# Rank of the first weight conversions, engine of the 1 / rms steps of pairs two and three, and lead of the first w3 loads

## Chip, core and metric
One core of a Trainium2 chip runs the whole program. The metric is device time in microseconds (us) of one execution, given as the median of several. Engines are TensorE (PE, with PEld for its weight loads), VectorE (DVE), ScalarE (ACT), GpSimd (POOL) and SyncE (SP, which only issues DMAs here). ScalarE and GpSimd issue DMAs as well.

## The reference
Inputs of the attention are float32, weights float64. `x` below is the attention output with the heads side by side, 1792 x 768.

```
q_n, k_n = rmsnorm(q, g_q), rmsnorm(k, g_k)      # x / sqrt(mean(x*x) + 1e-6) * g
attn = softmax(q_n @ k_n.T / sqrt(64)) @ v       # 4 batches, 12 heads, 448 rows, head size 64
h = x @ w_in;  x = maximum(0.01 * h, h) @ w_out  # 768 -> 2048 -> 768
a, b = x @ w1, x @ w2                            # 768 -> 1024 each
out = ((a * b) @ w3) @ w_last                    # 1024 -> 1024 -> 768
```

`w_last` is the second MLP's `w_out`. The kernel reads the weights as pairs of 32-bit words.

## The kernel before
Every matmul operand is split into a rounded part and a rest (`wh` and `wl`, `kh` and `kl`, `lasth` and `lastl`), and a product is three matmuls. The heads of a batch are worked in 24 pairs. For a pair t, `statistics(t)` makes 1 / rms of q and k: a square and a sum, `rs` by logarithm and exponential on ScalarE, and one small correcting step (lines 160 to 164 on GpSimd, lines 166 to 169 on VectorE for pair zero alone); line 174 then scales the keys. `keys(t)` transposes them (`pk`, L220) and splits them into `kh` (ScalarE, L229) and `kl` (VectorE, L230). `scores(t)` multiplies queries and keys into banks `ps` (L128), VectorE scales a bank and takes its minimum (L265), and ScalarE takes the exponential (L274). The results `p` are transposed into `pt` (L308), copied out as `pth`, and multiplied with the values (`po`).

Between these steps the two last weight matrices are multiplied with each other, w3 @ w_last, by `combine_weights` (banks `pw`, L554). It needs eight tiles of w_last and sixteen half tiles of w3. `Weights` brings them in this order: w_last 0 to 3 (tiles 0 to 3 of its list), the first w3 half (tile 4), then by turns a w_last tile and a w3 half (tiles 5 to 8), w_last 6 and 7 (tiles 9 and 10), and the remaining w3 halves. The first product needs tiles 0 to 4.

Conversion of a tile (`to_float32`) is two ScalarE passes over the words in place (L470, L474) and two VectorE passes into `raw` (L472, L476). `split` then makes hi and lo: for w_last on GpSimd (`lasth` L110, `lastl` L199), for w3 on ScalarE and VectorE (`wh` L505, `wl` L199). Words of w_last lie in a pool of four buffers, those of w3 in a pool `cv3` of five. `Weights.__init__` decides behind which tile's split a load is issued: as early as the buffer allows, and at most seven tiles ahead. A load issued after the first conversion goes to ScalarE's queue, an earlier one to SyncE's.

The order of instructions on each engine is fixed at build time by a list scheduler: among the work that is ready in its own estimate, the one with the higher priority goes first. Code within `tc.high_priority(n)` is ranked n places up: scores 600, statistics 100, and conversions `CONVERT_PRIORITY` = 100 (0 for the very first). On the chip each engine then works through its queue in that order, and waits at each instruction for its inputs and buffers.

Of the kernel before, what the change touches and what calls it, by code (L numbers as in the profile page):

```python
# [28 lines left out]
PB = 2  # L29
KH2 = K2 // 2  # L30
PARTIAL = 3
NO = DM // P
NH = B * H
NS = 1.0 / 2.4
CONVERT_NS = 500.0
CONVERT_PRIORITY = 100
STATS_AHEAD = 2
KEYS_AHEAD = 1
P_TILES = 8
TOGETHER = 2000  # L40
# [9 lines left out]
def attention_then_moe(  # L50
# [90 lines left out]
    def statistics(t):  # L141

        if t >= NH // 2:
            return
        x = pairs[t].pop("rows")
        ss = small.tile([CP, 2, 2, NCH], F32, tag="ss", name="ss", bufs=2)
        after = exps.get(t - STATS_AHEAD) or start.get("keys")
        for part in (1, 0):
            y = x[:, part]
            if part:  # L150
                y = bank("sq")[:CP].rearrange("p (h c d) -> p h c d", h=2, c=NCH)
            with tc.issue_after(after.ins) if after else ExitStack():
                nc.scalar.activation(y, x[:, part], AF.Square)
            nc.vector.tensor_reduce(ss[:, part], y, axis=AX.X, op=ALU.add)
        rs = small.tile([CP, 2, 2, NCH], F32, tag="rs", name="rs", bufs=4)
        y = small.tile([CP, 2, 2, NCH], F32, tag="y", name="y", bufs=2)
        nc.scalar.activation(y, ss, AF.Ln, scale=1.0 / D, bias=eps)
        nc.scalar.activation(rs, y, AF.Exp, scale=-0.5)
        if t:
            nc.gpsimd.tensor_scalar(ss, ss, 0.5 / D, 0.5e-6, op0=ALU.mult, op1=ALU.add)  # L160
            nc.gpsimd.tensor_tensor(y, rs, rs, op=ALU.mult)
            nc.gpsimd.tensor_tensor(y, y, ss, op=ALU.mult)
            nc.gpsimd.tensor_scalar(y, y, 1.0, -1.5, op0=ALU.mult, op1=ALU.add)
            nc.gpsimd.tensor_tensor(rs, y, rs, op=ALU.mult)
        else:
            nc.vector.tensor_scalar(ss, ss, 1.0 / D, 1e-6, op0=ALU.mult, op1=ALU.add)
            nc.vector.scalar_tensor_tensor(y, rs, 0.5, rs, op0=ALU.mult, op1=ALU.mult)
            nc.vector.tensor_tensor(y, y, ss, op=ALU.mult)
            nc.vector.scalar_tensor_tensor(rs, y, -1.5, rs, op0=ALU.add, op1=ALU.mult)
        pairs[t]["scale"] = rs[:, 0]  # L170
        kn = x[:, 0].rearrange("p h c d -> p (h c d)")
        kn = pairs[t]["kn"] = kn.rearrange("p (c h d) -> p c h d", c=NCH, h=2)
        rk = rs[:, 1].unsqueeze(3).to_broadcast([CP, 2, NCH, D])
        nc.vector.tensor_tensor(kn.rearrange("p c h d -> p h c d"), x[:, 1], rk, op=ALU.mult)
# [229 lines left out]
    class Weights:  # L404
# [9 lines left out]
        def __init__(self, sources):  # L414
            self.sources = sources
            self.raw, self.words, self.parts = {}, {}, {}
            self.ready = self.taken = 0
            self.rounded = None
            self.home, self.loads = {}, {}
            last = {"cv": [-4] * 4, "cv3": [-4] * 5}  # L420
            for t, (src, wide, _, _) in enumerate(sources):
                if wide:
                    home = self.home[t] = "cv3" if t < K2 * 3 and self.size(t) < DM else "cv"
                    after = max(last[home].pop(0), t - 7, -4 if t < 5 else 0)
                    self.loads.setdefault(after, []).append(t)
                    last[home].append(t)
            self.pieces = self.work()
            self.after = None
# [102 lines left out]
        def pump(self):  # L531

            if self.after and self.ready == len(self.sources):
                self.after.pump()
            elif self.ready - self.taken < self.AHEAD:
                with tc.high_priority(CONVERT_PRIORITY if self.ready else 0):
                    next(self.pieces, None)

        def take(self):
            while self.ready <= self.taken:  # L540
                with tc.high_priority(CONVERT_PRIORITY if self.ready else 0):
                    next(self.pieces)
            self.taken += 1
            return self.parts.pop(self.taken - 1)
# [18 lines left out]
            yield 3 * n * NS  # L563


    def combine_order():

        early = list(range(KH2))
        late = list(range(KH2, K2))
        yield early, 0, 0  # L570
        for k in range(1, PARTIAL):
            yield [late.pop(0)], k, 0
        yield late, 0, 1
        for k in range(1, PARTIAL):
            yield [], k, 1
        for k in range(PARTIAL, K2):
            yield [], k, 0
            yield [], k, 1

    def combine_weights(ws, pool, hi, lo):  # L580
# [5 lines left out]
        for new, k, half in combine_order():  # L586
            for _ in new:
                while ws.ready <= ws.taken:
                    with tc.high_priority(CONVERT_PRIORITY if ws.ready else 0):
                        next(ws.pieces)  # L590
                    yield CONVERT_NS
                ws.take()
# [159 lines left out]
    last = {}  # L752
# [402 lines left out]
```

## Time and profile before

| | us |
|---|---|
| median of 3 runs | 1183.69 |
| lowest and highest of the 3 | 1180.28 and 1185.77 |
| the profiled execution, its own time | 1182.5 |
| its span, first to last instruction | 1180.7 |
| TensorE busy in the span | 1137.4 |
| VectorE, ScalarE, GpSimd busy | 710.1, 657.7, 243.6 |

The span is the stretch that the trace shows; 1.8 us of the execution's own time lie outside it. An engine that is busy for nearly the whole span sets the time, and what it waits for in the rest is where time can come or go. A timeline row ends, where the engine stood idle before it, with the idle time and the instruction that ended it in brackets.

### The profile page before, as it was taken

What the parts mean: (1) busy time and instruction counts of PE and PEld (TensorE: products, weight loads), DVE (VectorE), ACT (ScalarE), POOL (GpSimd) and SP (SyncE); (2) the same over time, 40 slices, a digit from 0 to 9 for tenths busy, and PEclk for the clock granted to TensorE, in tenths of its full rate; (3) what the DMA queues carried; (4) which work ended last, traced back from release to release, by engine and by line L of the source; (5) the groups of instructions that cost most, each with busy time, mean ns of one, the idle gap of its engine ahead of it and who ended that gap; (6) DMA issues with size and microseconds to landing.
All of it is one profiled execution on the core that took longest, in us unless ns stands there. A gap on an engine that the chain in (4) does not pass through costs nothing.

```text
span 1180.7 us, 16739 instructions
## 1 busy us (share of the span) xinstructions
PE 1137.4 (96%) x6096; PEld 956.8 (81%) x6096; DVE 710.1 (60%) x1334; ACT 657.7 (56%) x1347; POOL 243.6 (21%) x345
## 2 busy tenths in 40 slices
PE   3899999999999999999999999999999999899998
PEld 2678867677787888888888888879999999699997
DVE  7986776877423667567545643483445556954553
ACT  6978687987534566676556643354443344443331
POOL 5632344544212232345222011000000000000000
PEclk8799999999999999999999999999999999999999
DMA  9556565985865446346332421440212212102112
GB/s 315 182 176 221 174 204 193 326 279 186 292 209 162 153 139 206 127 138 200 123 120 95 161 87 43 143 151 28 81 51 57 69 41 78 55 29 89 55 36 103
DMA packets 74979, 164.51 MB, mean 139 GB/s; under 512 B 13968, under 2 KB 42384, under 8 KB 74896
## 3 DMA queue, kind: packets, MB, share of 16 engines
q1 hardware_dynamic: 55392, 80.06, 22.5%
q10 hardware_dynamic: 10800, 48.76, 12.3%
q0 software_dynamic: 8704, 34.61, 7.8%
q8 instruction: 48, 0.79, 0.3%
q14 instruction: 35, 0.29, 0.1%
HBM read 120.46 MB, written 42.95 MB: 138 GB/s over the span
## 4 chain that ended last, share of the span: by engine, by line
PE 84%; DVE 7%; ACT 4%; DMA 3%; issue 1%; ACTq 0%; SPq 0%; POOL 0%; DVEq 0%; POOLq 0%
PE ps_mm L554 32%; PE ps_o L554 13%; PE ps_b L554 9%; PE pt L308 6%; PE ps L128 6%; PE po L128 6%; PE ps_c L554 5%; PE pw L554 5%; PE ps_a L554 2%; DVE ol L199 1%; DMA wh<-kept_first_mlp_h 1%; ACT p L274 1%; DVE wl L199 1%; PE pk L220 1%; ACT w L474 1%
## 5 line engine op out<-in xcount | busy, mean ns | idle before, releaser
L199 DVE TENSOR_TENSOR wl<-raw,wh 128x512 fp32r<-128x512 f32 (+1 forms) x136 | 109.4, 807 | 112.4 <-ACT wh L505 73.5
L265 DVE TENSOR_SCALAR_CACHE_REDUCE p<-ps,rs 112x448 f32<-112x448 f32 x192 | 122.2, 680 | 42.4 <-PE ps L128 42.4
L554 PE MATMUL ps_mm<-xl,wh 128*128 128x448 f32 x384 | 146.2, 381 | 0.0
L554 PE MATMUL ps_mm<-xh,wh 128*128 128x448 f32 x384 | 141.3, 368 | 2.3 <-DMA wh<-kept_first_mlp_h 2.3
L274 ACT ACTIVATE p<-p,low 112x448 f32<-112x448 f32 x192 | 126.5, 662 | 30.1 <-DVE p L265 29.8
L554 PE MATMUL ps_mm<-xh,wl 128*128 128x448 f32 x384 | 141.5, 368 | 0.7 <-DMA wl<-kept_first_mlp_l 0.7
L554 PE MATMUL ps_mm<-gl,wh 128*128 128x448 f32 x288 | 109.5, 381 | 0.0
L554 PE MATMUL ps_mm<-gh,wl 128*128 128x448 f32 x288 | 105.6, 367 | 1.6 <-DMA wl<-kept_first_mlp_l 1.6
L554 PE MATMUL ps_mm<-gh,wh 128*128 128x448 f32 x288 | 106.0, 369 | 1.1 <-DMA wh<-kept_first_mlp_h 1.0
L554 PE MATMUL ps_o<-gl,wh 128*128 128x448 f32 x288 | 104.3, 366 | 0.0
L554 PE MATMUL ps_o<-gh,wl 128*128 128x448 f32 x288 | 100.8, 366 | 0.0
L308 PEld LDWEIGHTS pt<-ident,p 112*112 112x112 f32 x768 | 82.2, 136 | 21.3 <-issue 7.1
L554 PE MATMUL ps_o<-gh,wh 128*128 128x448 f32 x288 | 99.4, 366 | 0.0
L470 ACT ACTIVATE w<-w 128x768 f32<-128x768 f32 (+1 forms) x80 | 63.4, 792 | 64.6 <-DMA w<-w_out 29.7
L308 PE MATMUL pt<-ident,p 112*112 112x112 f32 x768 | 96.2, 265 | 0.0
L505 ACT ACTIVATE wh<-raw 128x512 fp32r<-128x512 f32 (+1 forms) x84 | 59.2, 706 | 56.5 <-PE ps_mm L554 52.6
L554 PEld LDWEIGHTS ps_mm<-xl,wh 128*128 128x128 f32 x384 | 72.4, 189 | 12.5 <-issue 7.2
L476 DVE CUSTOM_DVE_ANT_0 raw<-w,raw 128x1024 uint16<-128x1024 uint16 (+1 forms) x80 | 79.2, 995 | 2.2 <-ACT w L474 0.5
L554 PEld LDWEIGHTS ps_mm<-xh,wh 128*128 128x128 f32 x384 | 72.3, 188 | 9.4 <-issue 3.7
L784 ACT ACTIVATE wh<-raw 128x512 fp32r<-128x512 f32 (+1 forms) x52 | 36.3, 698 | 76.3 <-PE ps_b L554 33.7
L554 PEld LDWEIGHTS ps_mm<-xh,wl 128*128 128x128 f32 x384 | 72.6, 189 | 7.6 <-issue 1.6
L128 PE MATMUL po<-pth,v_sb 112*64 112x448 f32 x384 | 77.5, 545 | 0.0
(141 smaller groups left out, 2530.5 us busy)
## 6 DMA issues: line engine op xcount, KB each, us to landing
w<-w_in ACTq DMA_DIRECT2D x16, 768.0 KB, 5.8
w<-w_out ACTq DMA_DIRECT2D x24, 512.0 KB, 3.9
w<-w ACTq DMA_DIRECT2D x16, 768.0 KB, 4.5
qk_sb<-qk SPq DMA_DIRECT2D x48, 224.0 KB, 4.0
w<-w3t ACTq DMA_DIRECT2D x15, 512.0 KB, 4.6
kept_first_mlp<-raw POOLq DMA_DIRECT2D x16, 384.0 KB, 4.3
kept_first_mlp<-raw POOLq DMA_DIRECT2D x24, 256.0 KB, 3.2
kept_second_mlp<-raw POOLq DMA_DIRECT2D x16, 384.0 KB, 2.9
```

Of the source, the lines that this page charges most:

```text
L128: one = nc.tensor.matmul(out, a, x, start=begin, stop=end)
L199: e.tensor_tensor(out, x, y.bitcast(F32), op=ALU.subtract)
L220: nc.tensor.transpose(pk[:, c * CP : (c + 1) * CP], kn[:, c].rearrange("p h d -> p (h d)"), ident[:CP, :CP],)
L265: nc.vector.tensor_scalar(p, ps[c % 2][e], x["scale"][:, e, c : c + 1], None, op0=ALU.mult, op1=ALU.min, accum_out=low,)
L274: exps[t] = nc.scalar.activation(p, p, AF.Exp, bias=low, scale=-1.0, accum_out=x["sums"][:, e, c : c + 1])
L308: nc.tensor.transpose(pt[:, c * CP : (c + 1) * CP], h["p"][c][:, kc * CP : (kc + 1) * CP], ident[:CP, :CP],)
L470: nc.scalar.activation(h, h, AF.Prelu, scale=2.0**-112, alpha=2.0**32)
L474: self.rounded = nc.scalar.activation(low, low, AF.Copy, scale=2.0**-29)
L476: nc.vector.tensor_tensor(top, top, low, op=ALU.add)
L505: self.rounded = nc.scalar.activation(flat[0], x, AF.Copy)
L554: nc.tensor.matmul(ps[:, :n], a, x, start=begin, stop=end, skip_group_check=on)
L784: nc.scalar.activation(parts[0], x, AF.Copy)
```

## The change
Three things change, and with them the build-time order of the engines' queues.

1. `words_first` ranks the conversions of the first five tiles (`ready <= KH2`, tiles 0 to 4) 1000 places up, above the scores' 600. Before, tile 0 had 0 and the others 100.
2. The correcting step of 1 / rms runs on VectorE for pairs zero, one and two (`POOL_SCALES = 3` counts pairs from zero), before only for pair zero. For the two pairs five GpSimd instructions each become four on VectorE.
3. Loads of the w3 tiles 4, 6 and 8 are issued at most four tiles ahead rather than seven. Tile 4 thereby leaves SyncE's queue, where it stood second among the weight loads, for ScalarE's.

Lines of the attention part move down by 3, those of `Weights` by 4, later ones by up to 7.

```diff
--- before.py
+++ after.py
@@ -29,12 +29,15 @@
 PB = 2
 KH2 = K2 // 2
 PARTIAL = 3
+LATE_WORDS = 4
 NO = DM // P
 NH = B * H
 NS = 1.0 / 2.4
 CONVERT_NS = 500.0
 CONVERT_PRIORITY = 100
+FIRST_WORDS = 1000
 STATS_AHEAD = 2
+POOL_SCALES = 3
 KEYS_AHEAD = 1
 P_TILES = 8
 TOGETHER = 2000
@@ -156,7 +159,7 @@
         y = small.tile([CP, 2, 2, NCH], F32, tag="y", name="y", bufs=2)
         nc.scalar.activation(y, ss, AF.Ln, scale=1.0 / D, bias=eps)
         nc.scalar.activation(rs, y, AF.Exp, scale=-0.5)
-        if t:
+        if t >= POOL_SCALES:
             nc.gpsimd.tensor_scalar(ss, ss, 0.5 / D, 0.5e-6, op0=ALU.mult, op1=ALU.add)
             nc.gpsimd.tensor_tensor(y, rs, rs, op=ALU.mult)
             nc.gpsimd.tensor_tensor(y, y, ss, op=ALU.mult)
@@ -421,7 +424,8 @@
             for t, (src, wide, _, _) in enumerate(sources):
                 if wide:
                     home = self.home[t] = "cv3" if t < K2 * 3 and self.size(t) < DM else "cv"
-                    after = max(last[home].pop(0), t - 7, -4 if t < 5 else 0)
+                    ahead = LATE_WORDS if home == "cv3" and t <= 2 * PARTIAL + 2 else 7
+                    after = max(last[home].pop(0), t - ahead, -4 if t < 5 else 0)
                     self.loads.setdefault(after, []).append(t)
                     last[home].append(t)
             self.pieces = self.work()
@@ -533,12 +537,12 @@
             if self.after and self.ready == len(self.sources):
                 self.after.pump()
             elif self.ready - self.taken < self.AHEAD:
-                with tc.high_priority(CONVERT_PRIORITY if self.ready else 0):
+                with tc.high_priority(words_first(self)):
                     next(self.pieces, None)
 
         def take(self):
             while self.ready <= self.taken:
-                with tc.high_priority(CONVERT_PRIORITY if self.ready else 0):
+                with tc.high_priority(words_first(self)):
                     next(self.pieces)
             self.taken += 1
             return self.parts.pop(self.taken - 1)
@@ -562,6 +566,9 @@
             ws.pump()
             yield 3 * n * NS
 
+
+    def words_first(ws):
+        return FIRST_WORDS if ws.ready <= KH2 else CONVERT_PRIORITY
 
     def combine_order():
 
@@ -586,7 +593,7 @@
         for new, k, half in combine_order():
             for _ in new:
                 while ws.ready <= ws.taken:
-                    with tc.high_priority(CONVERT_PRIORITY if ws.ready else 0):
+                    with tc.high_priority(words_first(ws)):
                         next(ws.pieces)
                     yield CONVERT_NS
                 ws.take()
```

How the queues move is shown at three places. Names with a number after `w_` are weight words; line numbers of the change are the new ones.

VectorE before, from the first scaled scores of pair zero to the scaled keys of pair one (last row):

```order
L265 TENSOR_SCALAR p,low<-ps,rs 112x448 x3
L472 TENSOR_SCALAR raw<-w_299 128x768
L476 ISA raw<-w_299,raw 128x1536
L265 TENSOR_SCALAR p,low<-ps,rs 112x448 x2
L174 TENSOR_TENSOR qk_sb<-qk_sb,rs 112x2x4x64
```

VectorE of the change, the last rows ahead of the scaled keys of pair one (the last two small steps are the rows with `y<-y,ss` and `rs<-y,rs`):

```order
L480 ISA raw<-w_300,raw 128x1536
L171 TENSOR_TENSOR y<-y,ss 112x16
L476 TENSOR_SCALAR raw<-w_302 128x768
L268 TENSOR_SCALAR p,low<-ps,rs 112x448 x2
L172 SCALAR_TENSOR_TENSOR rs<-y,rs 112x16
L480 ISA raw<-w_302,raw 128x1536
L177 TENSOR_TENSOR qk_sb<-qk_sb,rs 112x2x4x64
```

The scaled keys of pair one now stand behind all eight scaled scores of pair zero, behind the conversions of tiles 0 to 3 and behind the four small steps; before they stood behind six scaled scores and tiles 0 and 1.

VectorE before, the rows up to the low part `kl` of pair one's keys (last row):

```order
L476 ISA raw<-w_301,raw 128x1536
L472 TENSOR_SCALAR raw<-w_303 128x768
L472 TENSOR_SCALAR raw<-w_305 128x512
L476 ISA raw<-w_303,raw 128x1536
L476 ISA raw<-w_305,raw 128x1024
L230 SCALAR_TENSOR_TENSOR kl<-pk,gqk,kh 128x448
```

VectorE of the change, the rows between tile 4's conversion and the same `kl` (last row):

```order
L286 TENSOR_SCALAR r<-sum 112x8
L287 RECIPROCAL r<-r 112x8
L157 TENSOR_REDUCE ss<-qk_sb 112x8
L157 TENSOR_REDUCE ss<-sq 112x8
L476 TENSOR_SCALAR raw<-w_355 128x768
L111 COPY pth<-pt 112x448
L480 ISA raw<-w_355,raw 128x1536
L202 TENSOR_TENSOR wl<-raw,wh 128x512
L476 TENSOR_SCALAR raw<-w_461 128x512
L169 TENSOR_SCALAR ss<-ss 112x16
L480 ISA raw<-w_461,raw 128x1024
L233 SCALAR_TENSOR_TENSOR kl<-pk,gqk,kh 128x448
```

Tile 4's conversion (`w_305` before, `w_353` now) is still ahead of `kl`. New ahead of it are the two reciprocal rows, two sums, tiles 5 and 6, a copy `pth`, a rest `wl`, and a small step of pair two.

ScalarE before, around the high part `kh` of pair one's keys (`kh<-pk,gqk`):

```order
L274 ACTIVATE p,sum<-p,low 112x448 x2
L470 ACTIVATE w_303<-w_303 128x768
L474 ACTIVATE w_303<-w_303 128x768
L106 ACTIVATE qh<-qt_sb 128x448
L229 ACTIVATE kh<-pk,gqk 128x448
L274 ACTIVATE p,sum<-p,low 112x448 x2
L153 ACTIVATE sq<-qk_sb 112x512
```

ScalarE of the change, the rows that end with the same `kh`, after the squares of pair two:

```order
L156 ACTIVATE sq<-qk_sb 112x512
L474 ACTIVATE w_355<-w_355 128x768
L478 ACTIVATE w_355<-w_355 128x768
L509 ACTIVATE wh<-raw 128x512
L455 DMA w_483<-w3t 128x1024
L455 DMA w_488<-w3t 128x1024
L474 ACTIVATE w_461<-w_461 128x512
L478 ACTIVATE w_461<-w_461 128x512
L455 DMA w_556<-w3t 128x1024
L160 ACTIVATE y<-ss,eps 112x16
L109 ACTIVATE pth<-pt 112x448 x3
L232 ACTIVATE kh<-pk,gqk 128x448
```

Before, `kh` of pair one stood ahead of the squares of pair two (lines 153 before, 156 now); now it stands behind them, behind the words of tiles 5 and 6, a `wh` and three copies. On TensorE the products of `combine_weights` still begin behind the scores of pair one, in both programs.

## Rows read from the trace of the kernel before

**Rows 1.** Windows of the span: length, busy us of each engine, TensorE clock, DMA.
```profile
0.00:60.00 60.00, 36.36 (x174) 27.47 (x175) 50.52 (x84) 48.81 (x99) 34.28 (x36) 0.83 0.74 248
60.00:1181.00 1121.00, 1100.99 (x5924) 929.30 (x5922) 659.60 (x1251) 608.93 (x1249) 209.29 (x309) 1.00 0.41 133
```

**Rows 2.** Timeline of TensorE, rows with a wait: start, duration, wait.
```profile
21.59 0.98 PE L220 MATMUL pk<-ident,qk_sb 112*128 112x112 f32 x4 [5.77 <-ACT p L274]
...
30.52 0.71 PE L128 MATMUL ps<-kl,qh 64*112 64x448 f32 x2 [3.76 <-DVE kl L230]
...
33.24 0.66 PE L554 MATMUL pw<-lasth,wh 128*128 128x384 f32 x1 [0.34 <-ACT wh L505]
...
42.20 0.45 PE L554 MATMUL pw<-lasth,wh 128*128 128x384 f32 x1 [1.58 <-ACT wh L505]
...
46.88 0.69 PE L554 MATMUL pw<-lasth,wl 128*128 128x384 f32 x1 [2.17 <-DVE wl L199]
```

**Rows 3.** Windows, the two stretches after the first product at half clock.
```profile
33.24:37.00 3.76, 3.76 (x15) 3.56 (x16) 3.76 (x9) 3.76 (x9) 1.14 (x2) 0.50 1.02 390
43.80:50.70 6.90, 4.73 (x16) 3.67 (x15) 6.70 (x10) 6.90 (x14) 2.92 (x3) 0.51 0.25 100
```

**Rows 4.** Timeline of VectorE around pair one: start, duration, instruction.
```profile
12.82 0.56 DVE L472 TENSOR_SCALAR raw<-w 128x768 uint32<-128x768 uint32 x1
...
13.90 0.95 DVE L476 CUSTOM_DVE_ANT_0 raw<-w,raw 128x1536 uint16<-128x1536 uint16 x1
...
29.79 0.67 DVE L230 SCALAR_TENSOR_TENSOR kl<-pk,gqk,kh 128x448 fp32r<-128x448 f32 x1
...
30.39 0.20 DVE L283 TENSOR_SCALAR r<-sum 112x8 f32<-112x8 f32 x1
...
32.42 0.68 DVE L265 TENSOR_SCALAR_CACHE_REDUCE p<-ps,rs 112x448 f32<-112x448 f32 x1
...
34.09 0.69 DVE L199 TENSOR_TENSOR wl<-raw,wh 128x512 fp32r<-128x512 f32 x1
...
35.56 0.42 DVE L472 TENSOR_SCALAR raw<-w 128x512 uint32<-128x512 uint32 x1
...
37.11 2.32 DVE L476 CUSTOM_DVE_ANT_0 raw<-w,raw 128x1024 uint16<-128x1024 uint16 x1
```

**Rows 5.** Timeline of ScalarE from 24 to 36 us.
```profile
24.09 0.61 ACT L229 ACTIVATE kh<-pk,gqk 128x448 fp32r<-128x448 f32 x1
...
29.06 0.60 ACT L153 ACTIVATE sq<-qk_sb 112x512 f32<-112x512 f32 x1 [3.06 <-DMA qk_sb<-qk]
...
30.89 0.92 ACT L470 ACTIVATE w<-w 128x768 f32<-128x768 f32 x1 [0.24 <-DVE r L284]
...
35.45 0.31 ACT L157 ACTIVATE y<-ss,eps 112x16 f32<-112x16 f32 x1
```

**Rows 6.** Timeline of VectorE: small steps, and rows that last long.
```profile
6.92 1.01 DVE L166 TENSOR_SCALAR ss<-ss 112x16 f32<-112x16 f32 x1 [1.19 <-ACT y L157]
7.84 0.16 DVE L167 SCALAR_TENSOR_TENSOR y<-rs 112x16 f32<-112x16 f32 x1
...
8.46 0.69 DVE L174 TENSOR_TENSOR qk_sb<-qk_sb,rs 112x512 f32<-112x512 f32 x1
...
25.78 4.09 DVE L476 CUSTOM_DVE_ANT_0 raw<-w,raw 128x1536 uint16<-128x1536 uint16 x2
...
43.90 2.32 DVE L174 TENSOR_TENSOR qk_sb<-qk_sb,rs 112x512 f32<-112x512 f32 x1 [1.67 <-POOL rs L164]
```

**Rows 7.** Timeline of GpSimd: two subtractions beside those long rows.
```profile
25.66 1.85 POOL L199 TENSOR_TENSOR lastl<-raw,lasth 128x768 fp32r<-128x768 f32 x1
...
43.84 1.83 POOL L199 TENSOR_TENSOR lastl<-raw,lasth 128x768 fp32r<-128x768 f32 x1
```

**Rows 8.** The line of the weight loads, 0 to 40 us: issue, and issue to landing.
```profile
L451 ACTq DMA_DIRECT2D w<-w_last x4: 334/355/444, 15.0 to 30.4; - x4
...
DMA to landing us min/median/max: 4.0/7.8/11.1
```

## The prediction

> **What bounds the kernel now.** I first split TensorE's time by windows [rows 1]: in the first 60 us it is busy for 36.36, after them for 1101.0 of 1121. From 60 us on it runs almost without a pause, and VectorE and ScalarE are busy for less of the time than TensorE is. So a microsecond that TensorE loses in the first 60 us is a microsecond of the span, unless one of the few later pauses takes it up; I count on none of them.
>
> Then I read TensorE's timeline in those 60 us for its waits [rows 2]: 5.77 us before the key transposes of pair one (21.59), 3.76 before the last part of pair one's first scores (30.52, for `kl`), 0.34 before the first product of w3 and w_last (33.24, for `wh`), then 1.58 and 2.17 before the second w3 tile (`wh`, then `wl`). The last granted clock windows after the first product that stand at half speed [rows 3] are from 33.24 to 37.0 and from 43.8 to 50.7: 3.76 and 4.73 us busy at 1.2 rather than 2.4 GHz, so 1.9 and 2.4 us lost, 4.25 together. Both follow pauses.
>
> What TensorE waits for is VectorE and ScalarE: they are busy for 50.52 and 48.81 of the first 60 us [rows 1], with words to convert and scores to scale in one queue each. Every instruction put ahead of `kl` or `kh` in those queues comes out as lateness of the first product, since in both programs the products stand behind the scores of pair one.
>
> **The change part by part.**
>
> *Rank of the first five conversions.* The four w_last tiles and the first w3 tile now go ahead of the scores and of all that follows from them. The scaled keys of pair one fall behind two more scalings, tiles 2 and 3 and four small steps. A tile is 0.56 and 0.95, a scaling about 0.68, a small step about 0.2 (three from 7.84 to 8.46) [rows 4, 6]: 2 x 1.51 + 2 x 0.68 + 0.8 = 5.2, and with neighbouring rows overlapping by 0.07 (29.79 + 0.67 against 30.39 [rows 4]) about 4.7. So the transposes move from 21.59 to about 26.3. That alone is covered: behind them stand the 16 transposes of `p`, under 5 us at the pace of the four key transposes (0.98 [rows 2]), and TensorE then waits for `kh` and `kl` anyway.
>
> The path goes through `kl`. VectorE has these rows newly ahead of it: reciprocals, sums and one copy, 30.39 to 32.42 before, 2.03; tile 5, 1.51; one `wl`, 0.69; tile 6, 0.42 + 0.63 (the 0.95 of a wide tile cut to its two thirds); five small steps, 1.0 [rows 4, 6]. Sum 6.3, less 0.4 of overlap: 5.9, so `kl` would begin at 29.79 + 5.9 = 35.7. Before, it began at 29.79.
>
> ScalarE gives the same date by another way. `kh` stood at 24.09; now it stands behind the squares of pair two, the words of tiles 5 and 6, a `wh`, a logarithm and three copies. Before, that very sequence ran from 29.06 to 35.45 + 0.31, with its first row waiting 3.06 for the q and k rows of pair two [rows 5]. If these land as late as before, `kh` starts at about 35.7 and `kl` 0.6 behind it, 36.3. I take `kl` at 36.0, 6.2 later; the first product then moves from 33.24 to 39.4. **Lost: 6.2.** Bounds: VectorE's rows before `kl` were stretched by 2.5 us in one place alone (two L476 in 4.09 rather than some 1.5 [rows 6]). With that stretch gone the loss is 3.7; with two more such meetings of 1.8 it is 9.8.
>
> What is behind the first product gets better. Tiles 5 and 6 are converted by then: `wh` of tile 6 follows `kh` after two further w_last tiles on ScalarE, 35.7 + 0.6 + 2 x 1.7 = 39.7, and `wl` follows it on VectorE at about 40.5, while the 24 products of the first tile, which ran from 33.24 to 40.62 (42.20 less its wait), would last from 39.4 to 43.1 even in half that time [rows 2]. **Regained: the waits of 1.58 and 2.17, 3.75** [rows 2]. The half clock: after 30.52 TensorE stayed at half until 37.0, 6.5 us [rows 2, 3]. Restarted at 36.7 it would stay there until 43.2, of which 3.8 lie behind the first product: 1.9 lost in place of 4.25. **Regained: 2.3.** Bounds: nothing, if the next pause brings a second half-speed stretch; 4.25 if the restart is at full clock.
>
> *Small steps on VectorE.* For pair two the wait of VectorE for GpSimd (1.67 at 43.90) goes, and its scaled keys need no longer meet a subtraction on GpSimd (2.32 us there, from 43.90 to 46.2, beside a subtraction from 43.84 to 45.67 [rows 6, 7]); that is part of the 2.17 already counted. In its place five new rows per two pairs can meet one: the first step of pair zero took 1.01 and its siblings 0.16 [rows 6]. Behind the first product VectorE still has pair two's scaled keys, three tiles' words, a copy and a `wl` to do before the third w3 tile, and the copy frees a bank for the next scores. Nothing in the trace shows this order. From below such a wait is nothing, from above it is what two of the long rows cost beyond their own 0.6 and 1.5: 1.7 + 2.5 = 4.2 [rows 6]. I take 3.0, nearer the top, since GpSimd makes lo parts of tiles 7, 9 and 10 in just these microseconds. **New waits: 3.0.** The Trainium skill (SBUF — State Buffer, section "Who interferes with whom") says that a VectorE instruction with two SBUF inputs, or one in a two-port mode, is blocked by a GpSimd instruction for its whole length. The row of 2.32 us agrees. By that rule alone each step that meets a subtraction costs up to 1.8 us, and the rival below is its full case.
>
> *Loads.* Tile 4 is no longer loaded from SyncE but from ScalarE, at about 15 us (its first load there was at 15.0), and landings took 4.0 to 11.1 us, mostly 7.8 [rows 8]: 22.8. ScalarE comes to it at about 23.6 (24.09 less its own two passes of 1.1, which stood ahead, plus one exponential). Cost nothing, with 0.8 us of cover; without cover up to 2.5. All words are the same, so later pressure on the queues is unchanged.
>
> **Sum.** +6.2 - 3.75 - 2.3 + 3.0 = +3.2 us on an execution of 1182.5 with a span of 1180.7. The median of the three runs is 1183.7, 1.2 above that execution, so I expect **1187 us**, 0.3% slower. Half a per cent, 5.9 us, is about what a measurement of this kernel can tell from no change (its own three runs differ by 5.5).
>
> **The rivals.**
> - *All is regained.* As forecast, but VectorE is ready with the third tile in time: 6.2 - 6.05 = +0.2, 1184. For it: TensorE has two tiles' products, transposes and scores in that time. Chance 0.16.
> - *The port is the cost.* Three or four small steps or word passes more than before meet a GpSimd subtraction ahead of `kl`, 1.8 each, and the later copies too: +3.2 + 3 x 1.8 = +8.6, 1192. For it: the rows of 1.01 and 2.32. Against it: GpSimd's own ten small steps are gone. Chance 0.20.
> - *The other side: faster.* The stretch in VectorE's queue goes. Ahead of `kl` the two L476 met two GpSimd operations in a row, 2.5 us; the L472 and L476 before them were stretched by the same kind of meeting, and with GpSimd's steps gone they fall between subtractions. With `kl` at 32 (some 4 us sooner than I have it) the first product is at 35.4; 2.2 lost against 6.05 regained and no new wait give -3.9, 1180; with `kl` at 30, -5.9, 1178, which is where it decides. Against it: 5.9 us of rows are newly ahead of `kl`, and ScalarE's sequence holds `kh` as well. Chance 0.14.
> - *The first w3 words are late.* Landing after 11.1 us, ScalarE stands for 2.5 before tile 4, and so does all behind it: +5.7, 1189. Chance 0.06.
>
> **How the numbers follow.** The forecast has chance 0.44; its own range is 1184 to 1190 (the regained clock and the new waits at their bounds do not fall together). Of it a fifth lies over 1189.6, that is 0.09. Slower by over 0.5%: 0.09 + 0.20 x 0.9 + 0.03 = 0.30. Faster by over 0.5%: half of 0.14 and a little for the run's own spread, 0.09. Within: 0.61. The range that leaves out 2 in 10 goes from 1179, into the faster case, to 1194, past the port's.
>
> **What would show it.** Right: pair one's transposes on TensorE after 25 us, its `kh` after 33, the first product at 38 to 41; the waits before the second w3 tile gone; VectorE without a wait for GpSimd before pair two's scaled keys; busy time of TensorE in the first 60 us at 33 to 35 with later windows as before. Wrong: a first product before 36, or pauses of TensorE behind 60 us that before has and the change has not, or the reverse.

## The result and the profile after

| | before | after |
|---|---|---|
| median of 18 runs each, us | 1182.3 | 1188.82 |
| lowest and highest, us | 1178.23 and 1187.37 | 1185.32 and 1193.8 |
| profiled execution, own time and span, us | 1182.5, 1180.7 | 1187.53, 1185.7 |

The ratio after to before is 1.0068 (95% interval 1.0056 to 1.008): 8.0 us slower. The two medians of the table lie 6.5 us apart, a ratio of 1.0055, so the size is known to a microsecond or two. Forecast was +3.2 us, a median of 1187; it counted from the 1183.7 of the first three runs, 1.4 above the median of all 18. The profiled execution of after is a little under its median; its span is 5.0 us longer than that of before.

First TensorE's waits on its timeline after, to be read beside [rows 2]:

```profile
29.37 0.42 PE L223 MATMUL pk<-ident,qk_sb 112*128 112x112 f32 x1 [13.74 <-DVE qk_sb L177]
...
36.11 0.71 PE L131 MATMUL ps<-kh,qh 64*112 64x448 f32 x2 [2.77 <-ACT kh L232]
...
40.38 0.71 PE L131 MATMUL ps<-kl,qh 64*112 64x448 f32 x2 [3.19 <-DVE kl L233]
...
42.15 0.69 PE L558 MATMUL pw<-lasth,wh 128*128 128x384 f32 x1
42.64 0.52 PE L558 MATMUL pw<-lastl,wh 128*128 128x384 f32 x1
42.96 0.52 PE L558 MATMUL pw<-lasth,wl 128*128 128x384 f32 x1
...
44.19 0.34 PE L558 MATMUL pw<-lasth,wh 128*128 128x384 f32 x1
44.36 0.34 PE L558 MATMUL pw<-lastl,wh 128*128 128x384 f32 x1
...
51.40 0.46 PE L131 MATMUL ps<-kh,qh 64*112 64x448 f32 x1 [0.70 <-DVE pth L111]
...
58.97 0.60 PE L223 MATMUL pk<-ident,qk_sb 112*128 112x112 f32 x4 [2.21 <-DVE p L268]
```

The first product of w3 and w_last (L558, L554 before) comes at 42.15, before at 33.24: 8.9 us later. Neither `wh` nor `wl` is waited for behind it any more (1.58 and 2.17 before). New are 0.70 and 2.21, 2.9 together.

What holds that product back is `kl`. VectorE's timeline, the rows of the small steps (L169 to L172), the scaled keys (L177), the reciprocals' first row (L286) and `kl` (L233), beside [rows 4, 6]:

```profile
15.92 1.77 DVE L169 TENSOR_SCALAR ss<-ss 112x16 f32<-112x16 f32 x1
...
20.16 0.79 DVE L170 SCALAR_TENSOR_TENSOR y<-rs 112x16 f32<-112x16 f32 x1
...
23.55 0.16 DVE L171 TENSOR_TENSOR y<-y,ss 112x16 f32<-112x16 f32 x1
...
25.32 1.50 DVE L172 SCALAR_TENSOR_TENSOR rs<-y,rs 112x16 f32<-112x16 f32 x1
...
27.61 1.62 DVE L177 TENSOR_TENSOR qk_sb<-qk_sb,rs 112x512 f32<-112x512 f32 x1
...
30.71 1.79 DVE L286 TENSOR_SCALAR r<-sum 112x8 f32<-112x8 f32 x1
...
37.35 1.79 DVE L169 TENSOR_SCALAR ss<-ss 112x16 f32<-112x16 f32 x1
...
39.66 0.67 DVE L233 SCALAR_TENSOR_TENSOR kl<-pk,gqk,kh 128x448 fp32r<-128x448 f32 x1
```

A small step takes 0.16 us at 23.55, and 0.79, 1.50, 1.77 and 1.79 elsewhere; the reciprocals' first row (L286), 0.20 before, takes 1.79. `kl` stands at 39.66, before at 29.79. GpSimd's timeline shows what ran beside the long rows, beside [rows 7]:

```profile
15.66 2.00 POOL L202 TENSOR_TENSOR lastl<-raw,lasth 128x768 fp32r<-128x768 f32 x1
...
24.96 1.82 POOL L202 TENSOR_TENSOR lastl<-raw,lasth 128x768 fp32r<-128x768 f32 x1
26.74 1.92 POOL L202 TENSOR_TENSOR ql<-qt_sb,qh 128x448 fp32r<-128x448 f32 x1
...
30.33 2.14 POOL L202 TENSOR_TENSOR lastl<-raw,lasth 128x768 fp32r<-128x768 f32 x1
...
37.23 1.88 POOL L202 TENSOR_TENSOR lastl<-raw,lasth 128x768 fp32r<-128x768 f32 x1
```

Each long row of VectorE lies inside or across one of these subtractions: 15.92 in that of 15.66, 25.32 in 24.96, 27.61 in 26.74, 30.71 in 30.33, 37.35 in 37.23. The small steps among them (1.77, 1.50 and 1.79) and the L286 row end within 0.04 us of the end of the subtraction that they meet. The Trainium skill (SBUF — State Buffer, section "Who interferes with whom") says that a VectorE instruction in a two-port mode and a GpSimd instruction compete for a shared pair of ports: whoever issues first has it for its whole instruction, and the other is fully blocked. The trace agrees: steps of 1.77 and 1.79 beside subtractions of 2.00 and 1.88 that began 0.26 and 0.12 us earlier.

On ScalarE the words of tile 4 are converted without a wait for their load, and `kh` starts at 35.41 (forecast 35.7), beside [rows 5]:

```profile
25.49 0.65 ACT L474 ACTIVATE w<-w 128x512 f32<-128x512 f32 x1
...
35.41 0.65 ACT L232 ACTIVATE kh<-pk,gqk 128x448 fp32r<-128x448 f32 x1
```

Windows of after, with the busy time and number of instructions of each engine, then granted clock, DMA share and GB/s, beside [rows 1]:

```profile
0.00:60.00 60.00, 27.56 (x145) 22.07 (x146) 52.43 (x87) 45.61 (x89) 29.95 (x25) 1.00 0.74 245
...
780.00:1000.00 220.00, 217.68 (x1047) 197.87 (x1046) 117.14 (x193) 94.26 (x167) 0.00 (x0) 0.98 0.21 62
1000.00:1186.00 186.00, 176.77 (x844) 160.87 (x842) 106.92 (x179) 65.26 (x112) 0.00 (x0) 0.97 0.20 62
```

TensorE is busy for 27.56 of the first 60 us (36.36 before). But the kernel does not lose these 8.8 us for good: the last product of w3 and w_last starts at 160.44 against 157.04, 3.4 us later, and the last key transposes of the attention start at 690.53 against 688.05, 2.5 later. The other half of the 5.0 us comes behind 780, where TensorE runs at half clock more often. Windows of before, and then those of after that answer to them:

```profile
791.00:795.00 4.00, 4.00 (x13) 3.46 (x13) 3.35 (x6) 3.59 (x7) 0.00 (x0) 0.57 0.00 0
1013.00:1017.00 4.00, 4.00 (x12) 3.07 (x13) 4.00 (x8) 1.12 (x2) 0.00 (x0) 0.57 0.17 65
1021.00:1031.00 10.00, 9.30 (x42) 7.74 (x43) 9.10 (x17) 4.77 (x9) 0.00 (x0) 1.00 0.21 63
```

```profile
791.00:795.00 4.00, 3.01 (x7) 1.99 (x7) 2.99 (x6) 1.58 (x3) 0.00 (x0) 0.58 0.22 57
795.00:799.00 4.00, 4.00 (x13) 3.57 (x12) 3.31 (x5) 3.06 (x6) 0.00 (x0) 0.57 0.15 41
1016.00:1021.00 5.00, 4.69 (x15) 3.59 (x14) 5.00 (x10) 1.01 (x2) 0.00 (x0) 0.66 0.14 57
1023.00:1031.00 8.00, 7.21 (x20) 5.19 (x19) 5.48 (x10) 3.44 (x7) 0.00 (x0) 0.57 0.18 58
```

The clock column is the one ahead of the last two. Before, two stretches of 4 us stand at 0.57, and the one from 1021 at full clock; after, two of 4 us and one of 8 stand at 0.57 or 0.58, and one of 5 at 0.66.

### The profile page after: what moved, and what is told of

It is laid out like the page before. It is cut to its first block, busy times and chain, and to the rows that moved or that the text cites. A ratio compares the mean times of both kernels' runs of the same rounds, so it can differ in the third digit from the quotient of the medians.

```text
span 1185.7 us, 16731 instructions
## 1 busy us (share of the span) xinstructions
PE 1136.1 (96%) x6096; PEld 957.9 (81%) x6096; DVE 712.0 (60%) x1342; ACT 658.1 (56%) x1347; POOL 240.5 (20%) x335
## 4 chain that ended last, share of the span: by engine, by line
PE 82%; DMA 6%; DVE 5%; ACT 4%; issue 2%; SPq 0%; POOL 0%; ACTq 0%; DVEq 0%; POOLq 0%
PE ps_mm L558 32%; PE ps_o L558 13%; PE ps_b L558 10%; PE po L131 5%; PE pw L558 5%; PE pt L311 5%; PE ps_c L558 5%; PE ps L131 5%; PE ps_a L558 2%; DMA wl<-kept_first_mlp_l 1%; ACT p L277 1%; DVE ol L202 1%; DMA w<-w_last 1%; ACT w L478 1%; DMA w<-w_in 1%
## 5 line engine op out<-in xcount | busy, mean ns | idle before, releaser
L558 PE MATMUL ps_mm<-xl,wh 128*128 128x448 f32 x384 | 146.1, 380 | 0.5 <-POOL xl L202 0.5
L558 PE MATMUL ps_mm<-xh,wl 128*128 128x448 f32 x384 | 142.1, 370 | 2.2 <-DMA wl<-kept_first_mlp_l 2.2
L558 PE MATMUL ps_mm<-xh,wh 128*128 128x448 f32 x384 | 142.1, 370 | 0.0
L558 PE MATMUL ps_mm<-gl,wh 128*128 128x448 f32 x288 | 109.4, 381 | 0.0
L558 PE MATMUL ps_mm<-gh,wh 128*128 128x448 f32 x288 | 105.9, 369 | 0.5 <-DMA wh<-kept_first_mlp_h 0.5
L558 PE MATMUL ps_mm<-gh,wl 128*128 128x448 f32 x288 | 105.6, 367 | 0.9 <-DMA wl<-kept_first_mlp_l 0.9
L474 ACT ACTIVATE w<-w 128x512 f32<-128x512 f32 (+1 forms) x80 | 63.5, 794 | 75.7 <-DMA w<-w_out 32.4
L558 PE MATMUL ps_o<-gl,wh 128*128 128x448 f32 x288 | 104.2, 366 | 0.0
L558 PE MATMUL ps_o<-gh,wl 128*128 128x448 f32 x288 | 100.6, 366 | 0.0
L558 PE MATMUL ps_o<-gh,wh 128*128 128x448 f32 x288 | 99.2, 365 | 0.0
L558 PEld LDWEIGHTS ps_mm<-xl,wh 128*128 128x128 f32 x384 | 72.6, 189 | 11.8 <-issue 5.9
L558 PEld LDWEIGHTS ps_mm<-xh,wl 128*128 128x128 f32 x384 | 72.7, 189 | 9.8 <-DMA wl<-kept_first_mlp_l 2.4
L558 PEld LDWEIGHTS ps_mm<-xh,wh 128*128 128x128 f32 x384 | 72.4, 189 | 7.8 <-issue 2.1
L480 DVE CUSTOM_DVE_ANT_0 raw<-w,raw 128x1024 uint16<-128x1024 uint16 (+1 forms) x80 | 73.4, 920 | 2.4 <-ACT w L478 0.7
```

The lines of the kernel that those rows point to most:

```text
L474: nc.scalar.activation(h, h, AF.Prelu, scale=2.0**-112, alpha=2.0**32)
L480: nc.vector.tensor_tensor(top, top, low, op=ALU.add)
L558: nc.tensor.matmul(ps[:, :n], a, x, start=begin, stop=end, skip_group_check=on)
```

## The experiments

Ratios are against the kernel before, run in turn on the same chip (8 to 12 runs of each variant, 17 to 35 of before); the first row repeats the result above. "First product" and "last product" are the starts of the first and last matmul of w3 and w_last in the profiled execution, "`kl`" that of pair one; before has 29.79, 33.24 and 157.04.

| run | ratio, 95% interval | `kl` | first, last product |
|---|---|---|---|
| the whole change | 1.0068, 1.0056 to 1.008 | 39.66 | 42.15, 160.4 |
| `rank_only` | 0.9988, 0.9967 to 1.001 | 30.74 | 33.70, 157.6 |
| `steps_only` | 0.9983, 0.9963 to 1.0004 | 31.01 | 34.0, 156.4 |
| `loads_only` | 1.0041, 1.0018 to 1.0065 | 27.37 | 35.15, 164.4 |
| `rank_steps` | 1.0027, 1.0012 to 1.0042 | 30.01 | 33.0, 159.8 |
| `rank_loads` | 1.004, 1.0014 to 1.0066 | 36.44 | 38.94, 159.3 |
| `tile4_early` | 1.0046, 1.0028 to 1.0064 | 30.33 | 33.37, 159.6 |
| `tile4_late_only` | 1.0043, 1.0023 to 1.0063 | 37.25 | 39.7, 162.7 |
| `lo_in_four` | 1.0036, 1.0021 to 1.0052 | 37.83 | 40.3, 160.9 |
| `late_unswap` | 1.0036, 1.0014 to 1.0059 | 39.67 | 42.2, 160.4 |
| `four_unswap` | 1.0037, 1.002 to 1.0055 | 37.51 | 40.0, 158.5 |
| `late_swap` | 1.0004, 0.9984 to 1.0025 | 29.90 | 33.3, 157.1 |
| `steps_lo_in_four` | 0.9989, 0.9973 to 1.0005 | 28.23 | 32.7, 159.0 |

**The three parts, alone and in two of the three pairs.** Small steps with late loads, the third pair, was not run. The parts are undone in the changed kernel by these lines:

```diff
-LATE_WORDS = 4
+LATE_WORDS = 7          # no late loads
-POOL_SCALES = 3
+POOL_SCALES = 1         # small steps on GpSimd again
-        return FIRST_WORDS if ws.ready <= KH2 else CONVERT_PRIORITY
+        return CONVERT_PRIORITY if ws.ready else 0    # no rank
```

`rank_only`, as expected beforehand:

> The kernel before with the rank of the first five conversions alone (1000 over all else; small steps of pairs two and three stay on GpSimd, the first w3 words are loaded as before). Main theory (the queue): the first product of w3 and w_last goes where kl of pair one goes in VectorE's order, and the rank alone leaves kl behind the same rows as before (the words of tiles 3 and 4 directly ahead of it); so kl at 29 to 31 us, first product at 32.5 to 35, the waits of 1.6 and 2.2 us before the second w3 tile still there, ratio to the kernel before 0.998 to 1.002. Rival (the rank itself): conversions ahead of the scores delay pair one; kl at 35 or later, ratio 1.004 to 1.007. Rival (the port): no small steps on VectorE, so nothing is lost, as by the main theory; the two part in the run with rank and loads.

(Pairs two and three, counted from one, are the pairs one and two of the other texts.) The main theory held: `kl` at 30.74, first product at 33.70, ratio 0.9988. The rank costs nothing by itself that can be measured. The two waits before the second w3 tile are 0.82 and 1.48 here, and one of 2.06 is new at 53.95.

`steps_only`, as expected beforehand:

> The kernel before with the small steps of 1 / rms of pairs one and two on VectorE alone. Main theory (the queue): kl keeps its place behind the words of tiles 3 and 4, with four short rows more ahead of it; each that misses a GpSimd subtraction takes 0.16 us, each that meets one up to 1.8; kl at 30 to 32.5, ratio 0.999 to 1.002. Rival (the port): these steps carry most of the loss of the whole change, 6 to 8 us; kl at 33 to 35 with at least two steps of 1.4 us or more, ratio 1.003 to 1.007.

`kl` at 31.01, ratio 0.9983: nothing either, though here too scaled keys took 2.16 and two L480 4.10. The rival fell in this form: `kl` did not come at 33 or later.

`loads_only`, as expected beforehand:

> The kernel before with the late loading of the first w3 words alone (tile 4 is loaded from ScalarE, no longer from SyncE, and is converted after kl of pair one). Main theory (the queue): the two rows of tile 4 no longer stand ahead of kl, so kl at 27.5 to 29.5, about 1 us sooner; but the first product then waits for the words of tile 4 and its wh, and stands at 33 to 35.5 all the same; ratio 0.998 to 1.002. Rival (late words): tile 4 lands so late that ScalarE stands for it and the first product comes at 37 or later; ratio 1.003 to 1.006.

This one went against me. `kl` came early (27.37, just ahead of the range), and the first product at 35.15, as I expected; yet the kernel is 0.41% slower. TensorE's waits on its timeline:

```profile
35.15 0.66 PE L558 MATMUL pw<-lasth,wh 128*128 128x384 f32 x1 [1.20 <-issue]
...
46.47 0.45 PE L558 MATMUL pw<-lasth,wh 128*128 128x384 f32 x1 [3.17 <-ACT wh L509]
...
62.03 0.98 PE L311 MATMUL pt<-ident,p 112*112 112x112 f32 x8 [1.23 <-DVE ss L157]
...
68.04 0.93 PE L131 MATMUL ps<-kh,qh 64*112 64x448 f32 x2 [2.41 <-DVE kl L233]
```

The time is lost behind the first product. Tile 6, the second w3 tile, is not converted in time: TensorE stands 3.17 for its `wh` at 46.47 (1.58 and 2.17 in before, at 42.20 and 46.88). Then follow 1.23 and 2.41 around pair two, and the last product is 7.4 later. That VectorE and ScalarE have tiles left over there is my reading of these waits.

`rank_loads`, as expected beforehand:

> The whole change without its small steps (rank and late loads together; the small steps of pairs one and two stay on GpSimd). Main theory (the queue): only these two together put kl of pair one behind tiles 4, 5 and 6, a copy, the reciprocals and a wl on VectorE; kl at 36.5 to 39, first product at 39 to 42, no wait before the second w3 tile, ratio 1.004 to 1.007, nearly the whole loss. Rival (the port): the small steps on VectorE, five of them ahead of kl and up to 1.8 us each, are what made kl 9.9 us later and not 6.2; without them kl at 33 to 35.5, ratio 1.000 to 1.003.

VectorE's row of `kl`, and TensorE's rows of the last scores and the first product:

```profile
36.44 0.68 DVE L233 SCALAR_TENSOR_TENSOR kl<-pk,gqk,kh 128x448 fp32r<-128x448 f32 x1
```

```profile
37.17 0.71 PE L131 MATMUL ps<-kl,qh 64*112 64x448 f32 x2 [0.48 <-DVE kl L233]
...
38.94 0.69 PE L558 MATMUL pw<-lasth,wh 128*128 128x384 f32 x1
```

`kl` at 36.44 and the first product at 38.94 lie near what I had forecast for the whole change (36.0 and 39.4), though that forecast had 1.0 us of small steps in it. The small steps bring 3.2 us more of `kl` (39.66). The main theory came out in kind: both dates are 0.06 ahead of its ranges, no wait stands before the second w3 tile, and the ratio of 1.004 is at the lower end. But that is some 0.6 of the whole loss and not "nearly the whole", and the rival was right that the steps add about 3 us.

`rank_steps`, as expected beforehand:

> The whole change without its late loads (rank and small steps). Theory A (the loads are needed for the loss, rank and steps alone each cost nothing): kl behind tiles 3 and 4 at 30 to 32, first product at 33 to 35.5, ratio 0.996 to 1.001; if the gains of rank (0.9988) and steps (0.9983) add, 0.997. Theory B (the three parts add, and only noise hid it): ratio 1.002 to 1.004.

`kl` and the first product came early, as theory A says, but not the time: 1.0027, in theory B's range. The parts do not simply add, though: alone they gave 0.9988 and 0.9983. A date of the first product like that of before is not enough; here TensorE waits 3.79 for the second tile's `wh` at 43.51, and the last product is 2.7 later.

**Which late load.** In the condition of the loads:

```diff
-                    ahead = LATE_WORDS if home == "cv3" and t <= 2 * PARTIAL + 2 else 7
+                    ahead = LATE_WORDS if home == "cv3" and KH2 < t <= 2 * PARTIAL + 2 else 7   # tile4_early
+                    ahead = LATE_WORDS if home == "cv3" and t <= KH2 else 7                     # tile4_late_only
```

`tile4_early`, as expected beforehand:

> The changed kernel in which only tile 4, the first w3 tile, is again loaded as before (from SyncE, at the start); tiles 6 and 8 stay late, rank and small steps stay. Theory A (what matters in the loads is where tile 4 comes in: late, it drops behind the scaled keys of pair one, and tiles 5 and 6 with it go ahead of kl): kl is directly behind tiles 3 and 4 again, at 30 to 32, first product at 33 to 35.5, ratio 0.997 to 1.002. Theory B (late words in general: tiles 6 and 8 landing late cost it): ratio 1.003 or more, with waits before the second or third w3 tile longer than the 1.6 and 2.2 us of before.

`tile4_late_only`, as expected beforehand:

> The changed kernel in which only tile 4 is loaded late and tiles 6 and 8 as before. Theory A (tile 4): as the whole change, kl at 38 to 40.5, first product at 41 to 43, ratio 1.005 to 1.008. Theory B (tiles 6 and 8 matter as much): ratio 1.000 to 1.004.

Both cost about the same (1.0046 and 1.0043), so neither theory is the whole of it. With tile 4 early again the first product is back at 33.37, and the time is not. TensorE's timeline:

```profile
33.37 0.69 PE L558 MATMUL pw<-lasth,wh 128*128 128x384 f32 x1
...
44.33 0.69 PE L558 MATMUL pw<-lasth,wh 128*128 128x384 f32 x1 [3.79 <-ACT wh L509]
...
65.41 0.68 PE L131 MATMUL ps<-kh,qh 64*112 64x448 f32 x2 [1.83 <-DVE kl L233]
```

It now waits 3.79 for `wh` of the second w3 tile, and 1.83 for `kl` of pair two at 65.41. In these two runs late words hold back either the first product or the second tile.

**The port.** GpSimd's subtraction of the first four w_last tiles in four pieces:

```diff
-            subtract("V" if own else "P", flat[1], x, flat[0])
+            if t < KH2:
+                for c in range(0, n, n // 4):
+                    subtract("P", *(y[:, c : c + n // 4] for y in (flat[1], x, flat[0])))
+            else:
+                subtract("V" if own else "P", flat[1], x, flat[0])
```

`lo_in_four`, as expected beforehand:

> The changed kernel with each GpSimd subtraction of the first four w_last tiles (128 x 768) cut into four of 128 x 192; order on VectorE up to kl as in the changed kernel but for one copy. Theory A (the port: what the small steps add on top of rank and loads, 3.2 us of kl and 0.28% of the time, are meetings with a whole subtraction on GpSimd): a small step now waits for a quarter, 0.5 us or less, so kl at 36 to 37.8 in place of 39.7, first product at 38.5 to 40.5 in place of 42.1, ratio 1.003 to 1.0055. Theory B (the steps cost by their place in the queue, whatever GpSimd does): kl at 39 or later, ratio 1.006 to 1.008. If the pieces keep the port one after the other without a gap for VectorE, B's numbers come out too; then steps of 1.4 us and more are still there in the trace.

VectorE's small steps and `kl`, then GpSimd's subtractions (a row with x4 holds the four pieces together):

```profile
16.11 0.55 DVE L169 TENSOR_SCALAR ss<-ss 112x16 f32<-112x16 f32 x1
...
19.50 0.79 DVE L170 SCALAR_TENSOR_TENSOR y<-rs 112x16 f32<-112x16 f32 x1
...
22.30 0.56 DVE L171 TENSOR_TENSOR y<-y,ss 112x16 f32<-112x16 f32 x1
...
24.45 0.16 DVE L172 SCALAR_TENSOR_TENSOR rs<-y,rs 112x16 f32<-112x16 f32 x1
...
35.52 1.79 DVE L169 TENSOR_SCALAR ss<-ss 112x16 f32<-112x16 f32 x1
...
37.83 0.67 DVE L233 SCALAR_TENSOR_TENSOR kl<-pk,gqk,kh 128x448 fp32r<-128x448 f32 x1
```

```profile
20.36 3.41 POOL L202 TENSOR_TENSOR lastl<-raw,lasth 128x192 fp32r<-128x192 f32 x4
...
24.65 4.17 POOL L202 TENSOR_TENSOR lastl<-raw,lasth 128x192 fp32r<-128x192 f32 x4
...
35.41 1.88 POOL L202 TENSOR_TENSOR lastl<-raw,lasth 128x768 fp32r<-128x768 f32 x1
```

Steps beside pieces take 0.55, 0.79, 0.56 and 0.16 where they took 1.77, 0.79, 0.16 and 1.50. The one at 35.52 still takes 1.79: beside it stands the whole subtraction of tile 5, which is not cut. `kl` comes 1.8 earlier, as theory A says, and the ratio is 1.0036. GpSimd pays: of the four cut subtractions the four pieces last 2.43, 3.41, 4.17 and 3.41, a whole one 1.8 to 2.1 in the changed kernel; and VectorE now waits 1.59 for a `lastl` at 34.56.

`steps_lo_in_four`, the small steps alone with the same pieces, as expected beforehand:

> The best of the parts so far (the small steps of pairs one and two on VectorE alone, ratio 0.9983) with each GpSimd subtraction of the first four w_last tiles cut into four of 128 x 192. Theory A (the port): the meetings on VectorE ahead of kl of pair one get shorter by about 3 us (the two conversions of 4.10 together, the scaled keys of 2.16), kl at 27.5 to 29.5 in place of 31.0, ratio 0.994 to 0.998. Rival (kl is not what the time follows, something later takes the gain back): kl earlier, but ratio 0.998 to 1.001.

`kl` came at 28.23, 2.8 earlier than in `steps_only`, and bought nothing that can be measured: 0.9989. The rival held. TensorE waits 3.34 here for the second tile's `wh` (at 43.34), nearly as long as in `tile4_early` and `rank_steps`, and loses nothing by it. No run beat the kernel before by more than its measurement is uncertain.

**The late order.** The order of ScalarE's queue differs near 1018 us too: before, the copy `wh` goes ahead of a conversion `oh`, after, behind it, and TensorE waits 0.78 before and 1.62 after for it. The two runs make that swap in the kernel before, and undo it in the changed one (edits in part):

```diff
# late_swap, in the kernel before (block 60; last["t1"] is the conversion oh)
+            wait = last["t1"] if self.ready == 60 else None
+            with tc.issue_after(wait.ins) if wait else ExitStack():
                 nc.scalar.activation(parts[0], x, AF.Copy)
# late_unswap, in the changed kernel: that conversion is issued behind the copy
+            one = nc.scalar.activation(parts[0], x, AF.Copy)
+            if self.ready == 60:
+                with tc.issue_after(one.ins):
+                    two(*last["t1"])
```

`late_swap`, as expected beforehand:

> The kernel before with one late swap on ScalarE that the changed kernel also has (near 1018 us): the copy wh of the w_mlp block weights (wh from raw, 128x768) stands behind the conversion oh of the last difference of the operands, no longer ahead of it; its wl and some products of TensorE follow it. Nothing before 1010 us differs. Theory L (the late order costs what the first 60 us do not explain): from the last conversion of t (oh from t) to the end it takes 161.5 to 163 us as in the changed kernel (162.4), not 158.8 as before; ratio 1.002 to 1.0035. Rival (chance of the clock, or the swap is covered): 158.5 to 160.5, ratio 0.999 to 1.001.

ScalarE's and TensorE's timelines there, of the kernel before and then of `late_swap`:

```profile
1017.84 0.84 ACT L784 ACTIVATE wh<-raw 128x768 fp32r<-128x768 f32 x1 [2.30 <-PE ps_a L554]
1018.59 0.56 ACT L106 ACTIVATE oh<-acc 128x448 fp32r<-128x448 f32 x1
```

```profile
1018.73 0.47 PE L554 MATMUL ps_b<-oh,wh 128*128 128x448 f32 x1 [0.78 <-ACT wh L784]
```

```profile
1018.78 0.58 ACT L106 ACTIVATE oh<-acc 128x448 fp32r<-128x448 f32 x1 [2.80 <-DVE acc L867]
1019.27 0.83 ACT L786 ACTIVATE wh<-raw 128x768 fp32r<-128x768 f32 x1
```

```profile
1020.15 0.66 PE L554 MATMUL ps_b<-oh,wh 128*128 128x448 f32 x1 [1.83 <-ACT wh L786]
```

The swap does what was said: `wh` stands behind an `oh` that waits 2.80 for VectorE, and TensorE waits 1.83 rather than 0.78. The last stretch (from the last `oh` out of `t` to the end) takes 161.4 rather than 158.8. But over 12 runs that is 1.0004: theory L's price did not come out.

`late_unswap`, as expected beforehand:

> The changed kernel with that one late swap undone: the copy wh goes ahead of the conversion oh on ScalarE, and wl ahead of ol on VectorE; all else, the first 60 us too, as in the changed kernel. Theory L: the wait of TensorE for wh near 1022 us (1.62) shrinks to 0.8 or less, the last 160 us take 159 to 160.5 in place of 162.4, ratio 1.0035 to 1.0055. Rival (the late part does not matter, all of the loss is in the first 60 us): ratio 1.006 to 1.008.

The wait was 0.78 and the ratio 1.0036, as theory L says, but the last stretch still took 161.4, where it says 159 to 160.5.

`four_unswap`, as expected beforehand:

> The changed kernel with both remedies together: GpSimd's subtractions of the first four w_last tiles in four pieces, and the late swap of wh and oh undone. Each alone gave 1.0036. If the two are separate causes whose costs add (port 3.8 us, late order 3.8 us out of 8.0), ratio 0.999 to 1.002. If they are not (each run alone shows chance of the clock, or both buy back the same microseconds), 1.003 to 1.005. In the profile: first product near 40.3 as with the pieces alone, the last 160 us at 159 to 161.5.

1.0037, the same as with either remedy alone. So they are not two causes whose costs add, and the swap, which costs nothing in the kernel before, is not shown to be one at all.

**All runs together.** The eight kernels with late words, all three or some of them, have ratios of 1.0036 or more, and none of their intervals holds 1. The five without have 0.9983 to 1.0027, and only that of `rank_steps` is clear of 1. Without its late words the whole change falls from 1.0068 to 1.0027.

## Why the prediction was right, and where not

The sign was right and the time within the range; the forecast's +3.2 was 8.0 (6.5 by the plain medians), nearer to the +8.6 of the rival "The port is the cost". By its steps:

- **Lost: 6.2.** Measured 8.9. The place was right: `kl` sets the first product, and `kh` (35.41 for 35.7) does not. The transposes came at 29.37 and not 26.3, which was covered, as forecast. The term that was mis-sized most is the small steps. I counted the five that are newly ahead of `kl` at 1.0 us; the trace after shows them at 15.92, 20.16, 23.55, 25.32 and 37.35, with 1.77 + 0.79 + 0.16 + 1.50 + 1.79 = 6.0. That is the mechanism of the rival "The port is the cost", and its price of 1.8 a meeting. It is shown for `kl`: the same steps beside cut subtractions were shorter, and `kl` earlier. But `kl` did not move by all of it, since other terms were off too. Counted from start to start on VectorE, between pair zero's `kl` and pair one's, the change adds 5.6 for the steps, 3.7 for reciprocals, sums and copy (forecast 2.0), 0.9 for the scaled keys (forecast nothing) and 0.6 for `wl`; and the conversions, with tiles 5 and 6 more (forecast 2.6), take 10.7 in place of 11.5. In `rank_loads`, without the steps, the same conversions take 13.8. So the steps took over meetings with GpSimd that conversions have without them, and a meeting that moves from one row to another is not a new cost. That `kl` without the steps (36.44) stands so near the forecast is partly luck.
- **Regained: 3.75.** Right in the whole change: both waits are gone.
- **Regained: 2.3.** Behind the first product the matmuls follow each other by 0.32 us until 44.19 and by 0.17 from there on. The first pace is that of half clock, the second that of full clock (before, 0.32 in the half-clock stretch of [rows 3] from 47.36 on and 0.17 after 51.56). That is 2.0 us at half clock, 1.0 lost in place of 4.25: 3.2 regained.
- **New waits: 3.0.** Measured 0.70 + 2.21 = 2.9, but right by luck. I had put them down to the small steps. `rank_loads`, whose steps are on GpSimd, has the same two waits, 0.96 and 2.20, and `steps_only` neither. The 0.70 is for a copy `pth`, as forecast; the 2.21 is for scaled scores, and no product of w3 and w_last waits.
- **The sum.** With the measured terms it is 8.9 - 3.75 - 3.2 + 2.9 = +4.9. At the last product 3.4 are left: the rest was made good between the first and the last product, some of it in small pauses that are gone (0.51 us for `wo` at 67.31 before). That this stands near my +3.2 is partly luck, since the two terms Lost and Regained were off in opposite directions.
- **Loads: cost nothing.** This step failed. I priced only the landing of tile 4, and that was right (no wait at 25.49). What moves with it in the order I booked under the rank. The rank alone costs nothing, and `kl` goes behind tiles 5 and 6 only with rank and late loads together; but every variant with late words, wholly or in part, is 0.36% to 0.46% slower, also those whose first product is early. In `loads_only` the last product came 7.4 later, with waits of 3.17, 1.23 and 2.41 on the way.
- **"Each microsecond TensorE loses in the first 60 us counts".** Too simple, in both directions. TensorE was busy there for 27.56, not the 33 to 35 of the forecast, and the 8.8 us less became 3.4 by the last product. And `steps_lo_in_four` with its first product at 32.7, `tile4_early` at 33.4 and `loads_only` at 35.15 differ by 0.5% in time. The last product does not order the runs either: it is 1.9 later in `steps_lo_in_four`, which loses nothing, and 7.4 later in `loads_only`, which loses 0.41%. The profiled execution of `late_unswap`, with first and last product as late as in the whole change, spans 1179.0, less than the 1180.7 of before, while the median of its runs is 1186.9: the span of one profiled execution tells little of a change of this size.
- **Later windows as before.** Wrong. In the profile 2.5 of the 5.0 us come behind 690, with more stretches at half clock. Over all executions the mean granted clock has a median of 0.9825 in the 18 of after, and of 0.987 to 0.988 in the runs of before beside the experiments. Over 1181 us that is some 6 us, in which half-speed time of an idle TensorE counts too, and the first 60 us, whose clock reads 0.83 in the profile of before and 1.00 in that of after. So the number is no price of the late stretches: the profiled execution of after itself has a mean of 0.991, above the 0.987 of before.

**Left open.** Why the whole change has 1.0068 while the small steps left out (`rank_loads`), the cut subtractions, the late swap undone, and the last two together all give 1.0036 to 1.004. The interval of `lo_in_four` does not touch that of the whole change, but these comparisons were not all made on one chip, and by plain medians the whole change has 1.0055 and these four 1.003 to 1.005. How the late words come to cost their 0.4% is not shown either: neither product's date follows it. Nor is it known whether the rank is needed, since small steps with late loads were not run. What decides whether a pause near 790 or 1018 us is followed by a short or a long stretch at half clock was not found: one profiled execution for each kernel shows too few of them.

## To carry to other kernels

A step that is 0.16 us in one row can be 1.8 in the next if GpSimd subtracts beside it: the longest such row, times the number of GpSimd subtractions in the stretch, bounds what a move to VectorE costs from above; it is less where other VectorE rows met them already. When the order of a queue is worked out by a scheduler, parts of a change must be read together: here neither the rank nor the steps cost anything that could be measured alone. And a late input is not judged by one date in one profile: here neither the first product (33 to 42 us) nor the last (156 to 164 us) ordered the times of the kernels. Their executions did.

## What the runs showed of the hardware

- A GpSimd subtraction cut in four lets VectorE in between the pieces (steps of 0.55 and 0.56), and takes 2.43 to 4.17 us with VectorE at work beside it (`lo_in_four`), against 1.81 to 2.14 whole (the changed kernel).
- The clock column can be 1.00 where the clock is not full: after shows 1.00 for all of the first 60 us, while its matmuls of 384 columns follow each other by 0.32 us until 44.19 and by 0.17 afterwards. The pace of equal matmuls is the surer sign.
- Stretches at half clock late in the span differ between profiles with the same order of TensorE's instructions there: near 791 us, after the same two pauses of 0.95 or 0.96 and 0.99 us, that of `rank_loads` has none, that of `lo_in_four` one within 4 us, and that of the changed kernel one within 8 us.
